# Fused attention and two feed-forward blocks: tiles that share slots with the first mixing blocks, mixing products behind the last y, x in six stores

## The chip, the cores and the metric

The kernel runs on one core of a Trainium2 chip. A core has engines with queues of their own that work in order: PE (TensorE, matrix products), DVE (VectorE), ACT (ScalarE), POOL (GpSimd) and SP (SyncE), which here only issues DMAs. DMAs issued by any of them run on 16 shared DMA engines. The metric is the time of one execution on the device, in microseconds (us).

## The reference, cut to what matters

```python
def _attn_ref(q, k, v, beta):                     # 4 x 8 x 768 x 48
    k_n = k / (np.linalg.norm(k, axis=-1, keepdims=True) + 1e-06)
    state = zeros((B, H, D, D))
    for t in range(S):
        y[:, :, t] = einsum('bhd,bhde->bhe', q[:, :, t], state)
        v_old = einsum('bhde,bhd->bhe', state, k_n[:, :, t])
        state = state + beta_t * einsum('bhd,bhe->bhde', k_n[:, :, t], v_t - v_old)
    return y
def _moe_ref(x, w_in, g_ln, w_sg, b_sg, w_out):   # x: 4 x 768 x 384
    h = gelu_tanh(x @ w_in)                       # 1024 columns
    u, v = h[..., :512], h[..., 512:]
    v_n = (v - mean(v)) / sqrt(var(v) + 1e-06) * g_ln
    v_s = einsum('ts,bsd->btd', w_sg, v_n) + b_sg[None, :, None]
    return x + (u * v_s) @ w_out
def _moe2_ref(x, mu_k, mu_r, w_k, w_v, w_r):
    xk = mu_k * x + (1 - mu_k) * x_prev; xr = mu_r * x + (1 - mu_r) * x_prev
    return sigmoid(xr @ w_r) * (relu(xk @ w_k) ** 2 @ w_v)
```

The result is the second block applied to the first block applied to the attention's output, with the heads side by side as 384 columns.

## The kernel before

Line numbers are those of the kernel before, as the profile gives them; those of the changed kernel are named as such. Every large product is made of three: each operand is split into a rounded high part and a low part (`split`, L106: ACT makes the high part at L111, DVE or POOL the low part at L114), and high x high, high x low and low x high are added in PSUM.

**Attention.** The sequence is cut into 12 chunks of 64 tokens, s = 0 to 11; two chunks are a group g (6 groups). The 32 pairs of batch and head are worked on in two halves, o = 0 and 1. Each (s, o) passes six stages: st_rq (the state's products rk and qk), st_d0, st_l, st_d1 (a triangular solve in blocks, with the inverse DT and the gram GL; u is copied out at L482, SQ at L500), st_s (the new state, L509, copied into SQ at L515) and st_y (y, L523, copied into yst at L528). The two halves run three stages apart. SQ is one tile for each of o, parity of s and half h. `run()` (L808) issues the pieces of two stages, then two ticks of a planner, then units of feed-forward work on PE. In a tick the planner issues a few DVE operations of the solver of the next group, of layer norm, or of weight conversion (raw weights come in by SP, pass ACT L155, DVE, POOL L168, ACT L111 and POOL and go out again as wk_dh, wk_dl and others). PE, DVE, ACT and POOL work in the order in which the program is written here; SP's order is made by a scheduler.

**From y to the first block.** At odd s the y of a group is stored into xT by eight DMAs (`store_x` L539: four at L543, four at L547), from SP; for group 5 half of them are issued by ACT. Some ticks later (LAGX = 6) the group's x is split (xh, xl) and its units run on PE: `v_units` (L595, evacuated by ACT at L604, normalised at L631, stored as vn_d at L636) and `u_units` (L647, ug at L651, stored as u_d).

**Mixing.** Behind the attention's loop (L823) new pools are opened. w_sg is loaded in 12 tiles wst (L844) and split into ws0 (columns of the first half, t = 0) and ws1; v_n comes back from memory as vst (L856) and is split into a ring of 9 pairs vh, vl. This list `ahead` is worked off one item per turn of a loop in which the last group's units run too. Then, for each batch b and half t, 4 x 6 blocks c of three mixing products each (`mix_mm` L931; 72 per half), a gate with u (loaded back by L923; DVE w at L944 and L946, split into gh and gl) and the projection (L142). `begin` (L966) issues products of c = 0 to 4 of all four d of (0,0) first. In this stage `side` puts the conversions of w_r and w_v between the gates. The scheduler orders all engines but PE here.

**Channel mix.** The last part (from 544.85 us) is the second block: 1440 products L142 in a row.

Of the kernel before, what the change touches and what calls it, by code (L numbers as in the profile page):

```python
# [20 lines left out]
P = 128  # L21
# [10 lines left out]
SV = 60  # L32
B0 = 1.4
# [3 lines left out]
RUN = (3, 1, 2)  # L37
# [11 lines left out]
LAGX = 6  # L49
LAGU = 2  # L50
SHARE = ((1, 4, 1), (1, 3, 1), (2, 5, 1))
NRAW = 3
NGL = 3
# [24 lines left out]
def fused_kernel(  # L78
# [139 lines left out]
    fp = fl.enter_context(fp)  # L218
    with ExitStack() as at:
# [14 lines left out]
        kTb = [ap1.tile([P, NPR, C], F32, name=f"kT{i}") for i in range(NKT)]  # L234
# [32 lines left out]
        Dm = ap1.tile([P, 32, 32], F32, name="Dm")  # L267
# [5 lines left out]
        SQ = [[[ap1.tile([P, 8, D + C], F32, name=f"SQ{o}{i}{h}") for h in range(2)]  # L273
# [14 lines left out]
        def gram(g, parts=((0, 64),)):  # L288

            GD = ap1.tile([P, 32, NU], F32, name="GD")  # L290
            GL = ap2.tile([P, NU, 32], F32, name="GL", bufs=NGL)
            GLs[g] = GL
# [28 lines left out]
        def product(a_off, a_dims, a_t, b_off, b_dims, b_t):  # L321

            sh = [d[1] for d in a_dims]
            tmp = ap1.tile([P, 1024], F32, name="tmp")
# [4 lines left out]
        def solver(g):  # L329

            NT = ap1.tile([P, 32, 32], F32, name="NT")
# [79 lines left out]
            DT = ap2.tile([P, NU, 32], F32, name="DT")  # L411
# [105 lines left out]
        def st_y(s, o):  # L517
            g, cur = s // 2, SQ[o][s % 2]
            yps = bank()
            for p in range(8):  # L520
                for h in range(2):
                    b0 = 64 * h
                    T.matmul(yps[b0:b0 + 64, p, :], lhsT=cur[h][:, p, 0:64],  # L523
                             rhs=cur[h][:, p, D:], start=True, stop=True)
# [14 lines left out]
        def store_x(g, o, yst):  # L539
            ts_ = slice(1 + P * g, 1 + P * g + P)  # L540
            for h in range(2):
                for i in range(2):
                    (nc.scalar if g == NG - 1 and i else nc.sync).dma_start(out=xT[D * h:D * h + D, 2 * o + i, :, ts_],  # L543
                                      in_=yst[64 * h:64 * h + D, 4 * i:4 * i + 3, :])
            for h, e, n, blk, row in ((0, 0, 32, 0, 96), (0, 32, 16, 1, 96),
                                      (1, 0, 16, 1, 112), (1, 16, 32, 2, 96)):
                (nc.scalar if g == NG - 1 and h else nc.sync).dma_start(  # L547
                                  out=xT[row:row + n, 2 * o:2 * o + 2, blk, ts_],
                                  in_=yst[64 * h + e:64 * h + e + n, 3:8:4, :])
# [60 lines left out]
        def ln_steps(g, b, v):  # L610
# [7 lines left out]
            if b % n == n - 1:  # L618
# [11 lines left out]
                def apply(i):  # L630
                    A.activation(vs[b0 + i], vs[b0 + i], AF.Identity, bias=nm[:, i:i + 1],  # L631
                                 scale=rs[:, i:i + 1])
                    if (b0 + i, g) == (0, NG - 1):
# [155 lines left out]
        def tick():  # L789
# [7 lines left out]
            late = point[0] >= LATE  # L797
            if jobs and len(running) < RUN[1 + late] and n % (2 if late else EVERY) == 0:
# [9 lines left out]
        def run(*bodies):  # L808
# [3 lines left out]
            for _ in range(2):  # L812
                tick()
            fill(UNITS)

        for s in range(12):
            for i in range(6):
# [299 lines left out]
```

## Time and profile before

| | |
|---|---|
| median of 3 runs | 798.91 us (798.80 to 802.15) |
| the profiled execution | 801.47 us, of which the span of its trace is 799.8 us |
| mean granted clock of PE | 0.974 of full speed |
| busy share | PE 90%, DVE 66%, ACT 45%, POOL 25% |
| chain that ended last | PE 58%, DVE 14%, DMA 8%, ACT 4%, issue 3%, POOL 3%, SP's queue 3% |

The stages in the profiled execution: the last group's solver ends and step 10 begins near 318 us, the last y starts at 358.81, the last units end at 384.2, mixing runs from 388.66, the first projection starts at 420.43, and the channel mix runs from 544.85 to the end. A busy share says how long an engine had an instruction in it. The chain follows back from the last instruction what released it. In a timeline a bracket at a row's end tells how long the engine was idle before the row, and which operation ended that; ACTq and SPq are the engines' issuing of DMAs.

### The profile page before, as it was taken

To read this page: it belongs to the slowest core of one execution; us is meant where nothing else is said; L and a number is where in the kernel's file an instruction comes from. 1 tells how busy PE (TensorE), PEld (TensorE's weight loads), DVE (VectorE), ACT (ScalarE), POOL (GpSimd) and SP (SyncE) were. 2 spreads that over 40 slices of the span, in tenths; PEclk is the share of its full clock that TensorE was granted. 3 is DMA by queue.
4 is the path that set the end of the run, shared out by engine and by line. 5 is a ranking of instruction groups with operands and counts; after the bars stand their busy time and mean duration, and the time that the engine had idled before them with its cause. 6 is when DMAs were issued, how large, how long until landed. Compare 5 with 4: busy or idle time off the path is not lost.

```text
span 799.8 us, 23669 instructions
## 1 busy us (share of the span) xinstructions
PE 719.3 (90%) x10126; PEld 652.8 (82%) x10126; DVE 524.5 (66%) x1087; ACT 360.6 (45%) x732; POOL 201.4 (25%) x246
## 2 busy tenths in 40 slices
PE   3478898998988989977789989999999999999998
PEld 3335677777877877766779978999999999999998
DVE  6989679698697797334367786458855555553442
ACT  3225455555645656654534232116644544542331
POOL 3254333344332434533406444101000000000000
PEclk9979999999999999997989999999999999999999
DMA  8313344364453455435994645138200000000000
GB/s 240 76 49 87 99 113 127 106 166 147 109 152 122 114 150 161 143 118 179 311 329 158 226 153 164 40 103 220 64 20 30 11 20 31 11 20 31 11 21 30
DMA packets 84713, 89.19 MB, mean 112 GB/s; under 512 B 25600, under 2 KB 68736, under 8 KB 84608
## 3 DMA queue, kind: packets, MB, share of 16 engines
q1 hardware_dynamic: 78976, 78.25, 32.7%
q0 software_dynamic: 4736, 9.04, 4.1%
q8 instruction: 79, 1.29, 0.7%
q10 hardware_dynamic: 896, 0.39, 0.2%
q14 instruction: 26, 0.21, 0.1%
HBM read 56.86 MB, written 26.08 MB: 104 GB/s over the span
## 4 chain that ended last, share of the span: by engine, by line
PE 58%; DVE 14%; DMA 8%; ACT 4%; issue 3%; POOL 3%; SPq 3%; ACTq 0%; DVEq 0%; POOLq 0%
PE ms L142 34%; PE ms L931 6%; PE ms L647 3%; PE ms L595 3%; DVE tmp L326 3%; PE rk L435 3%; PE ms L523 2%; DMA raw<-in_w_v_dram 2%; POOL na L168 1%; PE sps L509 1%; PE ms L686 1%; PE rk L489 1%; SPq L547 1%; DMA vst<-vn_d 1%; PE ms L303 1%
## 5 line engine op out<-in xcount | busy, mean ns | idle before, releaser
L142 PE MATMUL ms<-wvh,sh 128*128 128x384 f32 x192 | 64.9, 338 | 0.0
L142 PE MATMUL ms<-wvl,sh 128*128 128x384 f32 x192 | 64.9, 338 | 0.0
L142 PE MATMUL ms<-wvh,sl 128*128 128x384 f32 x192 | 64.8, 338 | 0.0
L142 PE MATMUL ms<-xm_lo,wkh 128*128 128x384 f32 x192 | 64.2, 334 | 0.0
L142 PE MATMUL ms<-xm_hi,wkh 128*128 128x384 f32 x192 | 64.2, 334 | 0.0
L142 PE MATMUL ms<-xm_hi,wkl 128*128 128x384 f32 x192 | 64.1, 334 | 0.0
L427 DVE TENSOR_TENSOR r<-vk,rk 128x384 f32<-128x384 f32 x40 | 22.0, 550 | 60.7 <-PE rk L489 21.4
L475 POOL TENSOR_SCALAR_AFFINE_SELECT SQ<-SQ 64x512 f32<-64x512 f32 x48 | 36.5, 760 | 93.9 <-ACT SQ L474 92.1
L168 POOL TENSOR_TENSOR na<-na,raw 128x256 int32<-128x256 int32 (+2 forms) x43 | 37.6, 876 | 80.2 <-DVE na L166 52.5
L114 DVE TENSOR_TENSOR sl<-r,sh 128x384 fp32r<-128x384 f32 x64 | 35.6, 556 | 30.2 <-ACT sh L111 30.2
L435 PEld LDWEIGHTS rk<-r,DT 32*32 32x32 f32 x1536 | 35.3, 105 | 20.6 <-DVE r L427 10.6
L435 PE MATMUL rk<-r,DT 32*32 32x48 f32 x1536 | 41.8, 203 | 10.7 <-DVE r L427 9.5
L111 ACT ACTIVATE sh<-r 128x384 fp32r<-128x384 f32 x64 | 33.5, 524 | 35.7 <-DVE r L1037 35.7
L305 PE MATMUL ms<-kT 64*32 64x64 f32 (+1 forms) x896 | 31.6, 229 | 12.1 <-issue 12.1
L1053 DVE TENSOR_TENSOR ob<-th,ms 128x384 f32<-128x384 f32 x24 | 13.2, 552 | 43.4 <-PE ms L142 43.4
L1037 DVE TENSOR_TENSOR r<-r 128x384 f32<-128x384 f32 x64 | 35.3, 551 | 9.7 <-ACT r L1036 9.7
L595 PE MATMUL ms<-wiv_hi,xh 128*128 128x512 f32 x72 | 30.2, 439 | 12.2 <-ACT GL L312 6.0
L303 PE MATMUL ms<-kT 64*32 64x64 f32 (+1 forms) x896 | 31.2, 229 | 11.1 <-DMA kT<-in_kt_d_dram 7.1
L1036 ACT ACTIVATE r<-ms 128x384 f32<-128x384 f32 x64 | 30.7, 480 | 20.7 <-PE ms L142 20.0
L500 ACT ACTIVATE SQ<-rk 64x384 f32<-64x384 f32 x48 | 23.3, 485 | 35.8 <-PE rk L435 33.3
L647 PE MATMUL ms<-xl,wiu_hi 128*128 128x256 f32 x144 | 39.3, 300 | 0.0
L111 ACT ACTIVATE gh<-w 128x384 fp32r<-128x384 f32 x32 | 16.6, 521 | 50.3 <-DVE w L946 50.3
(160 smaller groups left out, 2268.7 us busy)
## 6 DMA issues: line engine op xcount, KB each, us to landing
kT<-in_kt_d_dram SPq DMA_DIRECT2D x12, 512.0 KB, 4.3
u_d<-ug SPq DMA_DIRECT2D x24, 256.0 KB, 2.8
u<-u_d SPq DMA_DIRECT2D x16, 384.0 KB, 4.7
vn_d<-v SPq DMA_DIRECT2D x23, 256.0 KB, 3.2
vst<-vn_d SPq DMA_DIRECT2D x23, 256.0 KB, 3.5
SQ<-in_q_d_dram SPq DMA_DIRECT2D x48, 96.0 KB, 3.7
vk<-in_vk_dram SPq DMA_DIRECT2D x24, 192.0 KB, 3.5
vk<-in_vk_dram SPq DMA_DIRECT2D x12, 384.0 KB, 4.3
```

What stands on the lines that cost most here:

```text
L111: A.activation(hi, src, AF.Copy)
L114: eng_lo.tensor_tensor(lo, src, hi.bitcast(F32), op=ALU.subtract)
L142: T.matmul(pt, lhsT=a, rhs=b, start=(i == 0), stop=(i == n - 1))
L168: G.tensor_tensor(a.bitcast(I32), a.bitcast(I32), w_lo.bitcast(I32), op=ALU.add)
L303: T.matmul(gps[r:r + 32, p, c0:c1], lhsT=t[r:r + 64, u, 0:32], rhs=t[r:r + 64, u, c0:c1], start=True, stop=True)
L305: T.matmul(gps[r + 32:r + 64, p, c0:c1], lhsT=t[r:r + 64, u, 32:64], rhs=vw2(t, r, 64, u * C + 32, [(0, (c1 - c0) // 32), (1, 32)]), start ...
L435: T.matmul(RQs[o][b0:b0 + 32, p, 0:D], lhsT=DT[b0:b0 + 32, u0 + p, :], rhs=t[b0:b0 + 32, p, :], start=True, stop=True, skip_group_check=True)
L475: G.affine_select(out=pt, in_=pt, pattern=[[0, 8], [1, C]], compare_op=ALU.is_gt, fill=0.0, base=0, channel_multiplier=-1)
L595: T.matmul(vstat[g, b], lhsT=a[:, c], rhs=w[:, c], start=first, stop=last)
L647: T.matmul(vstat["u"][:, 2 * P * d:2 * P * d + 2 * P], lhsT=w[:, c, ds_], rhs=a[:, c].rearrange("p b t -> p (b t)"), start=first, stop=last)
L931: T.matmul(pt[:, :DM], lhsT=v[:, ds_], rhs=w[:, c], start=(c == 0 and i == 0), stop=(c == 5 and i == 2))
L1037: V.tensor_tensor(r, r, r, op=ALU.mult)
```

## The change

The changed kernel opens the pool `wq` of the mixing stage before the attention, with six slots w0h0 to w0l2 (12 KB a partition in all for the halves of ws0) and five ring slots g0 to g4. In the attention two of the four kT, tiles of GL and DT, the pair SQ of o = 0 and even s, and NT, GD, Dm and tmp of the solver lie in these slots. From the second stage of step 10 on, the slots are given to ws0 and the ring: `early_items`, one per tick, load four w_sg tiles and the four v_n tiles c = 0 to 3 of batch 0, and from step 11 the last two w_sg tiles of ws0; each item is a load into one of two rotating staging tiles (st0, st1) in one tick and its split in the next (EARLY = 1). v of group 4 is split directly into the ring from its v unit, as that of group 5 was. The first two loads were put by the scheduler at SP's rows 29 and 30, at the program's start.

`begin(0, 0, 5)` now stands directly behind the last y, ahead of the last group's splits and units. x is stored by six DMAs instead of eight (y's columns are laid in another order in PSUM for it), and ACT issues only three of them, those of (5,1), h = 1. A third weight conversion may run from tick 118 on (RUN, LASTP), the lag of the last group's splits is 4 and 1 ticks (LAGE). wk is loaded in six DMAs into the slots of ws0, and some tiles of the channel mix use the ring's slots.

The diff, cut to its core:

```diff
+EARLY = 1
-RUN = (3, 1, 2)
+RUN = (3, 1, 2, 3)
+LAGE = (4, 1)
+LASTP = 118
...
+    wq = ctx.enter_context(tc.tile_pool(name="wq", bufs=1, side="right", reuse_waits="tile"))
+    W0 = [f"w0{x}{i}" for i in range(3) for x in "hl"]
+    G0 = [f"g{i}" for i in range(5)]
+    def slot(tag, shape, dtype=F32):
+        return wq.tile(shape, dtype, name="s" + tag, tag=tag)
+    sts = [(stg, "st0"), (stg, "st1")]
+    def turn(tiles, shape, dtype=F32):
+        tiles.append(tiles.pop(0))
+        pool, tag = tiles[-1]
+        return pool.tile(shape, dtype, name=tag, tag=tag, bufs=1)
+    def staged(src, n):
+        x = turn(sts, [P, HF])[:, 0:n]
+        nc.sync.dma_start(out=x, in_=src)
+        return x
...
-        kTb = [ap1.tile([P, NPR, C], F32, name=f"kT{i}") for i in range(NKT)]
+        kTb = [slot(W0[i], [P, NPR, C]) if i < 2 else ap1.tile([P, NPR, C], F32, name=f"kT{i}")
+               for i in range(NKT)]
...
+        NT, GD, Dm = (slot(x, [P, 32, 32]) for x in G0[:3])
+        tmp = slot(G0[3], [P, 1024])
+        GLb = [slot(G0[4], [P, NU, 32]), slot(W0[2], [P, NU, 32]),
+               ap1.tile([P, NU, 32], F32, name="GL")]
+        DTb = [slot(W0[3], [P, NU, 32]), ap1.tile([P, NU, 32], F32, name="DT")]
...
-                after(LAGX, lambda: splits.append((g, o)))
+                after(LAGX if g < NG - 1 else LAGE[o], lambda: splits.append((g, o)))
...
+            queues = (nc.sync, nc.scalar if o + g == NG else nc.sync)
             for h in range(2):
-                for i in range(2):
-                    (nc.scalar if g == NG - 1 and i else nc.sync).dma_start(out=xT[D * h:D * h + D, 2 * o + i, :, ts_],
-                                      in_=yst[64 * h:64 * h + D, 4 * i:4 * i + 3, :])
+                queues[h].dma_start(
+                    out=vw2(xT, D * h, D, 2 * o * 3 * (S + 1) + 1 + P * g, [(S + 1, 6), (1, P)]),
+                    in_=yst[64 * h:64 * h + D, 0:6, :])
...
             for _ in range(2):
                 tick()
+                if early_items:
+                    early_items.pop(0)()
             fill(UNITS)
+        def to_ring(b, c, vst):
+            t = turn(rb, [P, 2 * HF], F32R)
+            vh, vl = ring[b, c] = (t[:, 0:HF], t[:, HF:2 * HF])
+            split(A, G if c % 3 else V, vst, vh, vl)
+        def into(hl, src):
+            x = staged(src, DM)
+            yield
+            split(A, V, x, *hl)
+        def ahead_of(*items):
+            gens = [x for x in items]
+            q = []
+            def step():
+                if gens:
+                    q.append(gens.pop(0)())
+                    next(q[-1])
+                if len(q) > EARLY or not gens and q:
+                    next(q.pop(0), None)
+            return [step] * (len(gens) + EARLY)
...
         for s in range(12):
             for i in range(6):
+                if (s, i) == (10, 1):
+                    open_ring()
+                    open_ws(0)
+                    open_ws(1)
+                    early_items += ahead_of(*[lambda c=c: ws_in(c) for c in range(4)],
+                                            *[lambda c=c: v_in(c) for c in range(4)])
+                if (s, i) == (11, 0):
+                    open_ws(2)
+                    early_items += ahead_of(*[lambda c=c: ws_in(c) for c in (4, 5)])
...
-        for i in range(3, 6):
-            run(stages[i](11, 1))
+        run(stages[3](11, 1))
+        for f in early_items:
+            f()
+        run(stages[5](11, 1))
...
+    begin(0, 0, CS[0])
     while later or splits or units or streams or opened[0]:
```

Three places in the order, the rows of the kernel before first and then those of the changed one. Names are the program's tiles with a number for each use.

ACT in step 10 (half 0): SQ is the state's tile, st0 and st1 are the staging tiles, sw0h1 is the high part of w_sg tiles 2 and 3, g0 the ring's pair for v tile 0, raw a weight under conversion. Before:

```order
L155 ACTIVATE raw_5495<-raw_5495 128x256
L111 ACTIVATE raw_5495<-na_5716 128x256 [waits Pool_49]
L500 ACTIVATE SQ000_111<-rk_5517 64x8x48 [waits PE_49]
L500 ACTIVATE SQ001_112<-rk_5517 64x8x48
L474 ACTIVATE SQ100_115<-qk_5750 64x8x64 [waits PE_49]
L474 ACTIVATE SQ101_116<-qk_5750 64x8x64
L515 ACTIVATE SQ010_113<-sps0_101 48x8x48 [waits PE_49]
L515 ACTIVATE SQ011_114<-sps0_101 48x8x48
L482 ACTIVATE u1_5837<-rk_5749 128x384 [waits DVE_49,PE_49]
L604 ACTIVATE v_5844<-ms_5795 128x512 [waits PE_49]
```

After:

```order
L113 ACTIVATE raw_5351<-na_5581 128x256 [waits Pool_49]
L113 ACTIVATE sw0h1_5456<-st0_5587 128x384 [waits DMAHW4_49]
L523 ACTIVATE sw0h2_122<-rk_5372 64x8x48 [waits PE_49]
L523 ACTIVATE sw0l2_123<-rk_5372 64x8x48
L497 ACTIVATE SQ100_126<-qk_5623 64x8x64 [waits PE_49]
L497 ACTIVATE SQ101_127<-qk_5623 64x8x64
L157 ACTIVATE raw_5430<-raw_5430 128x256
L113 ACTIVATE sw0h1_5456<-st1_5595 128x384 [waits DMAHW7_49]
L113 ACTIVATE raw_5430<-na_5667 128x256 [waits Pool_49]
L113 ACTIVATE g0_5683<-st0_5673 128x512 [waits DMAHW3_49]
L538 ACTIVATE SQ010_124<-sps0_104 48x8x48 [waits PE_49]
L538 ACTIVATE SQ011_125<-sps0_104 48x8x48
```

Three splits that wait for DMAs have come between the copies; the first stands ahead of the two copies SQ of L500 (L523 after). Behind these rows follow u (L505 after), the splits of g1 and g2, and only then v (L627 after).

SP at the same place: xT<-yst are the last x stores of (4,1), vk and vn_d a load and a store of the attention. Before:

```order
L547 DMA xT_63<-yst_5283 16x2x128 [waits DMAHW1_49]
L547 DMA xT_63<-yst_5283 32x2x128 [waits DMAHW2_49]
L246 DMA vk_5705<-in_vk_dram 64x768 [waits DMAHW3_49]
L247 DMA vk_5705<-in_vk_dram 128x768 [waits DMAHW4_49]
L636 DMA vn_d_67<-v_5447 128x512 [waits DMAHW5_49,Activation_49]
L195 DMA wk_dh_71<-raw_5430 128x256 [waits DMAHW6_49]
L195 DMA wk_dl_72<-na_5634 128x256 [waits DMAHW7_49,Pool_49]
L195 DMA wk_dh_71<-raw_5495 128x256 [waits DMAHW0_49,Activation_49]
L195 DMA wk_dl_72<-na_5716 128x256 [waits DMAHW1_49,Pool_49]
L151 DMA raw_5839<-in_w_k_dram 128x512 [waits DMAHW6_49,DMAHW2_49,DVE_49]
L151 DMA raw_6104<-in_w_k_dram 128x512 [waits DMAHW3_49,DMAHW0_49,DVE_49]
```

After:

```order
L571 DMA xT_63<-yst_5146 32x2x128 [waits DMAHW0_49]
L268 DMA vk_5570<-in_vk_dram 64x768 [waits DMAHW1_49]
L269 DMA vk_5570<-in_vk_dram 128x768 [waits DMAHW2_49]
L659 DMA vn_d_67<-v_5305 128x512 [waits DMAHW3_49,Activation_49]
L237 DMA st0_5587<-in_w_sg_dram 128x384 [waits DMAHW4_49,DVE_49]
L197 DMA wk_dh_71<-raw_5289 128x256 [waits DMAHW5_49]
L197 DMA wk_dl_72<-na_5495 128x256 [waits DMAHW6_49,Pool_49]
L237 DMA st1_5595<-in_w_sg_dram 128x384 [waits DMAHW7_49,DVE_49]
L197 DMA wk_dh_71<-raw_5351 128x256 [waits DMAHW0_49,Activation_49]
L197 DMA wk_dl_72<-na_5581 128x256 [waits DMAHW1_49,Pool_49]
L153 DMA raw_5664<-in_w_k_dram 128x512 [waits DMAHW5_49,DMAHW2_49]
L237 DMA st0_5673<-vn_d_67 128x512 [waits DMAHW4_49,DMAHW3_49,DVE_49]
```

The load of st0_5587, which ACT's split sw0h1 waits for, stands behind the x stores, vk and vn_d; the next load into the same tile, st0_5673, waits for DVE's part of that split.

PE behind the last y: xh and xl are the split x of a group, ms the product's bank, wiv and wiu the input weights, sw0h0 and sw0l0 the parts of w_sg tile 0, g0 the ring's pair. Before:

```order
L523 MATMUL ms_6363<-SQ110_117 64x64
L523 MATMUL ms_6363<-SQ111_118 64x64
L595 MATMUL ms_6431<-wiv_hi_90,xh_6393 128x512 [waits Activation_49]
L595 MATMUL ms_6431<-wiv_hi_90,xh_6393 128x512 x2
L595 MATMUL ms_6431<-wiv_lo_91,xh_6393 128x512 x3
L595 MATMUL ms_6431<-wiv_hi_90,xl_6394 128x512 [waits DVE_49]
L595 MATMUL ms_6431<-wiv_hi_90,xl_6394 128x512 x2
```

After:

```order
L546 MATMUL ms_6273<-SQ110_128 64x64
L546 MATMUL ms_6273<-SQ111_129 64x64
L670 MATMUL ms_6266<-xl_5802,wiu_hi_95 128x256 x3
L670 MATMUL ms_6266<-xh_5801,wiu_hi_95 128x256 x3
L670 MATMUL ms_6266<-xh_5801,wiu_lo_96 128x256 x3
L670 MATMUL ms_6266<-xl_5802,wiu_hi_95 128x256 x3
L937 MATMUL ms_6355<-sw0h0_5454,g0_5683 128x384
L937 MATMUL ms_6355<-sw0l0_5455,g0_5683 128x384
L937 MATMUL ms_6355<-sw0h0_5454,g0_5683 128x384
L937 MATMUL ms_6356<-sw0h0_5454,g0_5683 128x384
```

Before, the v units of group 5 follow the y and wait for its xh. After, 12 u products of group 4 and 60 mixing products, without a wait, stand between the y and these units.

## Rows read from the trace of the kernel before

**Rows 1.** The page: an engine's busy us, share and instructions.

```profile
PE 719.3 (90%) x10126; PEld 652.8 (82%) x10126; DVE 524.5 (66%) x1087; ACT 360.6 (45%) x732; POOL 201.4 (25%) x246
```

**Rows 2.** Stretches: length, busy PE, PEld, DVE, ACT, POOL, clock, DMA share, GB/s.

```profile
320.00:340.00 20.00, 18.70 (x405) 15.87 (x404) 6.51 (x16) 12.14 (x25) 10.76 (x15) 1.00 0.50 144
...
358.80:388.60 29.80, 20.63 (x140) 18.37 (x140) 12.24 (x28) 15.48 (x30) 12.73 (x21) 0.83 0.68 201
388.60:420.60 32.00, 29.10 (x128) 26.09 (x129) 19.40 (x35) 13.03 (x27) 5.14 (x5) 0.84 1.01 330
```

**Rows 3.** PE timeline, last y to first projection: start us, us, instructions, [idle before].

```profile
358.81 1.98 PE L523 MATMUL ms<-SQ 128*64 128x64 f32 x32 [3.38 <-ACT ug L651]
365.68 1.65 PE L595 MATMUL ms<-wiv_hi,xh 128*128 128x512 f32 x3 [4.90 <-ACT xh L111]
...
369.37 0.85 PE L595 MATMUL ms<-wiv_hi,xh 128*128 128x512 f32 x3
...
371.44 0.52 PE L647 MATMUL ms<-xh,wiu_hi 128*128 128x256 f32 x3
...
375.75 0.86 PE L595 MATMUL ms<-wiv_hi,xh 128*128 128x512 f32 x3
...
388.66 0.44 PE L931 MATMUL ms<-ws0h,vh 128*128 128x384 f32 x1 [4.33 <-ACT vh L111]
...
420.43 0.33 PE L142 MATMUL ms<-gh,wo_hi 128*128 128x384 f32 x1
```

**Rows 4.** Chain of waits in order of time: start us, us, what.

```profile
528.19 16.66 PE ms L931 x96
544.85 251.56 PE ms L142 x1440
```

**Rows 5.** SP timeline in step 10.

```profile
317.78 2.74 SPq L543 DMA_DIRECT2D xT<-yst  x4
320.57 2.54 SPq L547 DMA_DIRECT2D xT<-yst  x4
...
325.20 0.37 SPq L636 DMA_DIRECT2D vn_d<-v  x1
```

**Rows 6.** ACT timeline in step 10.

```profile
321.17 0.99 ACT L500 ACTIVATE SQ<-rk 64x384 f32<-64x384 f32 x2
...
324.17 0.47 ACT L482 ACTIVATE u<-rk 128x384 f32<-128x384 f32 x1
324.63 0.60 ACT L604 ACTIVATE v<-ms 128x512 f32<-128x512 f32 x1
326.65 0.60 ACT L528 ACTIVATE yst<-ms 128x512 f32<-128x512 f32 x1 [1.42 <-PE ms L523]
...
332.00 1.00 ACT L500 ACTIVATE SQ<-rk 64x384 f32<-64x384 f32 x2 [1.79 <-PE rk L435]
```

**Rows 7.** DMA issues: KB each, median us from issue to landing.

```profile
u<-u_d SPq DMA_DIRECT2D x16, 384.0 KB, 4.7
...
vst<-vn_d SPq DMA_DIRECT2D x23, 256.0 KB, 3.5
...
wst<-in_w_sg_dram SPq DMA_DIRECT2D x12, 192.0 KB, 4.4
raw<-in_w_out_dram SPq DMA_DIRECT2D x8, 192.0 KB, 2.9
```

**Rows 8.** Groups by line: busy us, mean ns of one, idle before.

```profile
L111 ACT ACTIVATE vh<-vst 128x512 fp32r<-128x512 f32 x23 | 13.9, 628 | 22.0 <-DMA vst<-vn_d 16.2 <-PE ms L931 5.7
L114 DVE TENSOR_TENSOR ws0l<-wst,ws0h 128x384 fp32r<-128x384 f32 x6 | 5.1, 853 | 10.3 <-ACT ws0h L111 10.3
```

**Rows 9.** ACT timeline in step 11: the x stores that ACT issues for (5,0).

```profile
349.80 1.57 ACTq L543 DMA_DIRECT2D xT<-yst  x2
351.41 1.38 ACTq L547 DMA_DIRECT2D xT<-yst  x2
```

**Rows 10.** PE timeline in a middle group: PE's wait for r.

```profile
180.34 0.87 PE L435 MATMUL rk<-r,DT 32*32 32x48 f32 x32 [2.30 <-DVE r L427]
```

More of the change, by code (lines that the diff above doesn't have):

```diff
@@ L272, in fused_kernel @@
                         base=0, channel_multiplier=1)
-        SQ = [[[ap1.tile([P, 8, D + C], F32, name=f"SQ{o}{i}{h}") for h in range(2)]
+        SQ = [[[ap1.tile([P, 8, D + C], F32, name=f"SQ{o}{i}{h}") if o or i else
+                vw(slot(W0[4 + h], [P, 1024]), 0, [(D + C, 8), (1, D + C)]) for h in range(2)]
                for i in range(2)] for o in range(2)]
@@ L861, in load_v, with mix_mm, begin @@
         to_ring(b, c, vsts.pop((b, c)))
-        if b == 0 and c < 2:
-            fetch_v(0, c + 3)
-    def to_ring(b, c, vst):
-        vh = vr.tile([P, HF], F32R, name="vh")
-        vl = vr.tile([P, HF], F32R, name="vl")
-        split(A, G if c % 3 else V, vst, vh, vl)
-        ring[b, c] = (vh, vl)
-    ahead = []
-    for i in range(5):
-        ahead += [lambda i=i: load_ws(0, i), lambda i=i: load_v(0, i)]
-    ahead.append(lambda: load_ws(0, 5))
-    for c in range(3):
-        fetch_ws(c)
-        fetch_v(0, c)
-    ahead += [lambda i=i: load_ws(1, i) for i in range(6)]
+    def mix_mm(pt, b, t, d, c):
+        ds_ = slice(d * P, d * P + P)
+        vh, vl = ring[b, c]
+        wh, wl = wsl[t][c]
+        for i, (v, w) in enumerate(((vh, wh), (vh, wl), (vl, wh))):
+            T.matmul(pt[:, :DM], lhsT=v[:, ds_], rhs=w, start=(c == 0 and i == 0),
+                     stop=(c == 5 and i == 2))
+    begun = {}
+    def begin(b, t, n):
+        for d in range(4):
+            begun[d] = (ps.tile([P, HF], F32, name="ms"), n)
+        for c in range(n):
+            for d in range(4):
+                mix_mm(begun[d][0], b, t, d, c)
     nc.sync.dma_start(out=b_sb, in_=b_sg.partition_broadcast(P))
+    ahead = ahead_of(*[lambda c=c: into(wsl[1][c], w_sg[c * P:(c + 1) * P, DM:2 * DM])
+                       for c in range(6)])
+    begin(0, 0, CS[0])
     while later or splits or units or streams or opened[0]:
@@ L924, in load_u @@
                               in_=u_d[b // 2, e, :, :, b % 2, t * DM:t * DM + DM])
-    def mix_mm(pt, b, t, d, c):
-        ds_ = slice(d * P, d * P + P)
-        vh, vl = ring[b, c]
-        wh, wl = ws[t]
-        for i, (v, w) in enumerate(((vh, wh), (vh, wl), (vl, wh))):
-            T.matmul(pt[:, :DM], lhsT=v[:, ds_], rhs=w[:, c], start=(c == 0 and i == 0),
-                     stop=(c == 5 and i == 2))
     def mix(b, t, d):
@@ L963, in fused_kernel @@
     load_u(0, 1)
-    begun = {}
-    def begin(b, t, n):
-        for d in range(4):
-            begun[d] = (ps.tile([P, HF], F32, name="ms"), n)
-        for c in range(n):
-            for d in range(4):
-                mix_mm(begun[d][0], b, t, d, c)
     for k, (b, t) in enumerate(halves):
```

102 lines of the change are left out of this document (55 added, 47 removed).

## The prediction

> **What bounds the kernel now.** I read the page's busy shares first: TensorE (PE) is busy nine tenths of the span [rows 1], so a gain has to come out of the tenth in which it is not, or out of a low clock. The chain of waits comes second. From 544.85 us it is one piece of 251.56 us of PE channel-mix products [rows 4]; nothing in the diff adds or removes a matmul there, so that third of the span stays. The table by stretches comes third and says where PE loses: between the start of the last y (358.8) and the start of the first projection (420.4) PE has two stretches with a granted clock of 0.83 and 0.84, is busy 20.63 of 29.80 us in the first, and in the second the DMA engines are full (share 1.01, 330 GB/s) [rows 2]. The PE timeline tells what it waits for there [rows 3]: 4.90 us for the split xh of the last group's x, then 4.33 us for the first split vh of the mixing stage, and short waits for weight splits after that. From 358.81 to 420.43 are 61.6 us.
>
> How much of it is work? Rates at full clock: nine v products from 369.37 to 371.44 are 0.23 us each, 36 u products from 371.44 to 375.75 are 0.12 us each [rows 3], 96 mixing products in 16.66 us are 0.1735 us each [rows 4]. Before, the place holds the y, 36 v, 72 u, 72 + 54 mixing products: 2 + 8.3 + 8.6 + 21.9 = 40.8 us of work in 61.6 us. So 20.8 us are waits and half clock, and that is what there is to win.
>
> **Part 1: 60 mixing products behind the last y.** In the order of the changed kernel the y is followed by 12 u products left over from group 4, then 60 mixing products of (0,0) whose operands were split during steps 10 and 11, so that they wait for nothing. Under them the last x lands, and the last group's units follow without the 4.90 us wait; the ring is full when they end, so the 4.33 us wait goes too. After the y starts: y 2.0 at the half clock of its row; 12 u products, between 1.4 (full clock) and 2.9 (half), I take 2.5, nearest to the y ahead of them, which ran slow; 60 x 0.1735 = 10.4; v 8.3; u 8.6; 12 mixing products of c = 5, 2.1; 54 of (0,1), 9.4. Sum 43.3 us. Next late is the first gating: the last u units end 31.8 us after the y starts, their stores and the reload of u stand behind them on SP's queue, a u load lands 4.7 us after its issue [rows 7], and four gatings follow on DVE and ScalarE (ACT). That comes about when the projection wants it; bounds 0 and 4 us, taken 1.5. So 44.8 instead of 61.6: **-16.8 us** (bounds -18.3 and -14).
>
> **Part 2: what steps 10 and 11 pay for it.** Ten loads into two staging buffers and eleven splits (six w_sg tiles, five v tiles, the fifth straight from its v unit) now stand in the queues of the last two steps. Two w_sg loads are issued at the program's start and cost only their split. The third is the expensive one. On ACT its split stands directly ahead of the copies SQ (L500 before), which the next state product waits for. ACT came to these at 321.17 [rows 6]. But its load stands on SP behind all x stores of (4,1), two vk loads and a vn_d store. SP issued eight x stores from 317.78 to 323.11, 0.66 us each, and the vn_d store at 325.20 with 0.37 us [rows 5]; two stores fewer bring its end to 325.57 - 1.32 = 324.25. Landing takes 2.9 us for a load of the same size from memory in the quiet attention stage, 4.4 us in the crowded mixing stage [rows 7]. At 320 to 340 us the DMA share is 0.50 [rows 2], so I take 2.9: 327.15, and ACT stands from about 321.2 to there, **6.0 us** (7.5 by the other row). Queued behind it are SQ and all of step 10's copies; PE, which works in a fixed order, waits for SQ.
>
> After that the pace is that of two buffers. A buffer's next load is issued only after both halves of its last split: for a v tile, landing 3.5 [rows 7], ACT 0.63 and DVE about 0.85 [rows 8], with issue some 5.3 us for a round. Followed by hand through ACT's queue: SQ at 327.7 and the affine copies to 329.9, second w_sg tile split by 330.8, the converted weight 332.4 (its wait on GpSimd kept), g0 by 333.2, u (L482) 334.5 instead of 324.17 or +10.3, g1 lands 335.3 and is split by 336, g2 lands 337.7 and is split by 338.4, then v (L604) at 338.4, where it was 324.63 [rows 6]: +13.8. Of that, five splits are 2.9 us, the rest waits. The state chain itself carries the +10.3 into the second half of step 10 and meets g3 there ahead of its SQ: about +11 to +12. Step 11 inserts three more splits, 1.7 us, and loses four x stores that ACT issued for (5,0), 1.57 + 1.38 = 2.95 us [rows 9], of which about half was ahead of a wait for PE anyway: together 0. The clock was full at 320 to 340 [rows 2]; after waits of this kind PE ran at the lower level in other places of the trace (the 0.83 above), so I add 1.5 us. **+13 us** on the start of the last y (bounds +7, rival one, and +20).
>
> The Trainium skill, "DMA: Bandwidth & Descriptors", section "Rules for kernel authors", says to issue a DMA early and wait for it late, since its fixed cost then overlaps with compute; one tick between load and split is against that rule, and the 2.9 us of the row speaks for the rule. Its section on the anatomy of one DMA fits 2.0 us plus the bytes at 436 GB/s, for GpSimd's path: that is an estimate of 2.45 us for a w_sg load and 2.6 us for a v tile, and by it the four landings in a row would be some 3 us shorter together, and the sum 792.6.
>
> **Part 3: the rest.** Six x stores for eight: in the middle groups PE's long wait once a group is for DVE's residual r, 2.30 us [rows 10], not for x, so 0 there; in steps 9 and 10 it is counted above. The shared slots (solver, gram, keys): they are taken over only after the last solver and gram have run, 0. In the mixing stage the conversion of w_r and w_v now starts later against PE, since PE arrives earlier by its own clock; it already made PE wait a few us there. I add 0.5 (bounds -1 and +4). The split of wk into six loads and the changed buffers of the channel mix: 0, for PE was without a gap there [rows 4].
>
> **Sum**: -16.8 + 13 + 0.5 = -3.3 us. The profiled execution took 801.47 us, 2.56 over the median of 798.91, and would become 798.2; against the median, the time to predict is 795.6. With the bounds of parts 1 and 3 it may be 2 us lower or 6 higher, with the landing times of part 2 some 5 lower or higher; its own range is 790 to 801.
>
> **Rivals.** *One: the waits fall into idle time.* ACT idled 1.42 us and 1.79 us between 324 and 332 waiting for PE [rows 6] and PE had slack in its units; if the rounds after the first stall hide there, only the 6.0 us and about 1 us of splits stay: +7 instead of +13, 789.6; and if the third load came in time too, -16.3 + 1, about 783. For it: neither PE nor ACT is full there. Against it: the copies stand in one queue, and the load's place behind the x stores is read from the order. *Two, slower: landings as in the crowded stage.* The change puts ten loads of 192 to 256 KB into steps in which x, vk, wk and u also move; if each of the four rounds in a row lands after 5.0 us rather than 2.9 or 3.5, the loss is 13 + 4 x 1.9 = 20.6 us, net +4.3, 803.2, and any PE time at the lower clock comes on top. It decides from landings of about 4.2 us (no gain left) and 5 us (slower by more than can be told from nothing). For it the 4.4 us row, against it the share of 0.50. *Three: the mixing products don't start behind the y*, because g4 or the third pair of w_sg tiles comes later than the y. Then PE waits in front of 60 products with the units queued behind them: some 5 us, 800.6. Against it: their splits stand on ACT well ahead of the last yst.
>
> **How the numbers follow.** The forecast 0.53, rival one 0.24, rival two 0.15, rival three 0.08. About 4 us (0.5%) is what a measurement of this kernel can tell from no change: faster means under 794.9, slower over 802.9. Forecast: 0.22 of its 0.53 lie under 794.9, 0.28 between, 0.03 above; rival one is faster but for 0.01; rival two slower in 0.12, rival three in 0.03. Faster 0.45, same 0.37, slower 0.18. The range that leaves out a tenth on either side: 784 to 804.
>
> **What would show it.** Right: an ACT wait of about 6 us for DMA in front of the third w_sg split at 321 us, and smaller ones before g1 and g2; the last y starting 10 to 16 us later, near 372; from there to the first projection about 45 us with mixing products at 0.17 us right behind the u products; equal length from the first projection on. Wrong: the last y starting under 365 (rival one), after 378 (rival two), a wait in front of the 60 products (three), or a long wait of PE for gl or wo in front of the first projection, which I priced at 1.5 us.

## The result, and the profile after

The changed kernel is slower: 810.46 us (median of 4 runs, 807.55 to 812.64) against 799.0 us, a ratio of 1.0132 with a 95% interval of 1.0089 to 1.0174. I had predicted 795.6, with 784 to 804 as the range. The profiled execution took 809.45 us, 8.0 more than the profiled one of before.

The trace gives three pieces. From the copy of y (9,1) to the copy of the last y, that is over steps 10 and 11: 318.84 to 380.83 us, 61.99, where before it was 316.21 to 360.82, 44.61: **+17.4**. From there to the channel mix: 171.85 instead of 184.03, **-12.2**. Before y (9,1): **+2.6**. Together 7.8, of the 7.9 between the spans of the two traces (807.7 and 799.8). The copies that bound the pieces, of the kernel before and then of the changed one (start us, us, instruction):

```profile
316.21 0.60 ACT L528 ACTIVATE yst<-ms 128x512 f32<-128x512 f32 x1 [0.48 <-PE ms L523]
...
360.82 0.60 ACT L528 ACTIVATE yst<-ms 128x512 f32<-128x512 f32 x1 [0.97 <-PE ms L523]
```

```profile
318.84 0.60 ACT L551 ACTIVATE yst<-ms 128x512 f32<-128x512 f32 x1
...
380.83 0.60 ACT L551 ACTIVATE yst<-ms 128x512 f32<-128x512 f32 x1 [1.62 <-PE ms L546]
```

The first piece, in ACT's timeline of step 10 (start us, us, instruction, idle time before it and what ended it), which answers [rows 6]:

```profile
323.70 0.42 ACT L113 ACTIVATE raw<-na 128x256 fp32r<-128x256 f32 x1 [2.09 <-POOL na L170]
331.65 0.52 ACT L113 ACTIVATE sw0h<-st 128x384 fp32r<-128x384 f32 x1 [7.53 <-DMA st<-in_w_sg_dram]
332.20 0.49 ACT L523 ACTIVATE sw0h<-rk 64x384 f32<-64x384 f32 x1
...
336.51 0.42 ACT L113 ACTIVATE raw<-na 128x256 fp32r<-128x256 f32 x1 [1.21 <-POOL na L170]
...
341.07 0.63 ACT L113 ACTIVATE g<-st 128x512 fp32r<-128x512 f32 x1 [1.59 <-DMA st<-vn_d]
341.60 0.58 ACT L627 ACTIVATE v<-ms 128x512 f32<-128x512 f32 x1
344.06 0.60 ACT L551 ACTIVATE yst<-ms 128x512 f32<-128x512 f32 x1 [1.88 <-PE ms L546]
...
351.81 0.99 ACT L523 ACTIVATE SQ<-rk 64x384 f32<-64x384 f32 x2 [2.06 <-PE rk L458]
```

ACT stands 7.53 us in front of the third w_sg split, and the two copies SQ (here named by the slots in which they lie, sw0h and sw0l) wait behind it. SP's timeline answers [rows 5]; the load that ACT waits for is its last row here and landed 3.86 us after its issue by the chain:

```profile
322.06 1.29 SPq L566 DMA_DIRECT2D xT<-yst  x2
323.40 2.53 SPq L571 DMA_DIRECT2D xT<-yst  x4
325.97 0.59 SPq L268 DMA_DIRECT2D vk<-in_vk_dram  x1
326.61 0.58 SPq L269 DMA_DIRECT2D vk<-in_vk_dram  x1
327.30 0.38 SPq L659 DMA_DIRECT2D vn_d<-v  x1
327.77 0.38 SPq L237 DMA_DIRECT2D st<-in_w_sg_dram  x1
```

ACT was ready at 324.12 (323.70 + 0.42). So 3.65 of its 7.53 us passed before SP had come through six x stores, two vk loads and a vn_d store to this load, and 3.88 until the load had landed.

PE in the same place (the state product and the y of (10,0), and behind them one of the v products), and then the stretches as in [rows 2]:

```profile
332.74 0.39 PE L532 MATMUL sps<-sw0h,vk 64*48 64x48 f32 x2 [8.59 <-ACT sw0h L523]
342.23 0.27 PE L546 MATMUL ms<-sw0h 128*64 128x64 f32 x1 [3.21 <-ACT v L627]
...
346.39 0.63 PE L618 MATMUL ms<-wiv_hi,xh 128*128 128x512 f32 x1
```

```profile
320.00:340.00 20.00, 10.32 (x175) 7.62 (x173) 6.15 (x12) 8.47 (x18) 8.88 (x9) 0.74 0.69 203
340.00:360.00 20.00, 16.12 (x316) 14.54 (x318) 8.14 (x16) 9.59 (x19) 8.65 (x12) 0.82 0.25 77
```

From 320 to 340 us PE is busy 10.32 us of 20 where it was 18.70, and the granted clock of the two stretches is 0.74 and 0.82 where it was 1.00 and 0.97.

The second piece. From the last y on, the chain of waits (start us, us, what) runs without a hole through the products that were moved there and half of the v units; behind these it goes, with shorter pieces between them, through three DMAs. The second fence shows PE's waits at the first projection, from the PE timeline, the third the chain's last row:

```profile
379.36 1.44 PE ms L546 x32
380.80 2.83 PE ms L670 x12
383.63 10.41 PE ms L937 x60
394.03 4.09 PE ms L618 x18
...
404.15 4.95 DMA st<-in_w_sg_dram
410.26 6.15 DMA st<-in_w_sg_dram
418.05 5.91 DMA u<-u_d
```

```profile
425.86 0.44 PE L144 MATMUL ms<-gh,wo_hi 128*128 128x384 f32 x1 [1.38 <-ACT gh L113]
...
429.00 0.69 PE L144 MATMUL ms<-gh,wo_hi 128*128 128x384 f32 x1 [1.40 <-ACT gh L113]
```

```profile
552.68 251.56 PE ms L144 x1440
```

Start of the last y on PE (379.36) to first projection (425.86): 46.5 us where [rows 3] have 61.6. The channel mix takes the same 251.56 us as [rows 4].

### The profile page after: what moved, and what is told of

The parts are those of the page before. It is cut to its first block, busy times and chain, and to the rows that moved or that the text cites. A ratio compares the mean times of both kernels' runs of the same rounds, so it can differ in the third digit from the quotient of the medians.

```text
span 807.7 us, 23622 instructions
## 1 busy us (share of the span) xinstructions
PE 726.1 (90%) x10126; PEld 661.5 (82%) x10126; DVE 525.0 (65%) x1087; ACT 360.8 (45%) x732; POOL 204.8 (25%) x250
## 4 chain that ended last, share of the span: by engine, by line
PE 64%; DVE 11%; DMA 7%; ACT 5%; POOL 3%; issue 2%; SPq 1%; DVEq 0%; POOLq 0%; ACTq 0%
PE ms L144 34%; PE ms L937 8%; PE ms L618 4%; PE ms L670 3%; PE rk L458 3%; PE ms L546 2%; DVE sg L350 2%; DMA st<-in_w_sg_dram 2%; PE sps L532 2%; PE rk L512 2%; PE ms L709 2%; POOL na L170 1%; DMA raw<-in_w_v_dram 1%; PE rk L482 1%; PE ms L328 1%
## 5 line engine op out<-in xcount | busy, mean ns | idle before, releaser
L144 PE MATMUL ms<-xm_hi,sw0h 128*128 128x384 f32 x192 | 64.1, 334 | 0.0
L144 PE MATMUL ms<-xm_lo,sw0h 128*128 128x384 f32 x192 | 64.1, 334 | 0.0
L144 PE MATMUL ms<-xm_hi,sw0l 128*128 128x384 f32 x192 | 64.1, 334 | 0.0
L116 DVE TENSOR_TENSOR sl<-sg,sh 128x384 fp32r<-128x384 f32 x64 | 35.7, 558 | 30.3 <-ACT sh L113 30.2
L937 PE MATMUL ms<-ws1h,g 128*128 128x384 f32 x192 | 50.2, 335 | 1.5 <-ACT ws1h L113 1.5
L937 PE MATMUL ms<-sw0h,g 128*128 128x384 f32 x192 | 50.1, 335 | 0.0
L350 DVE TENSOR_TENSOR sg<-sg,Yt 128x512 f32<-128x512 f32 (+10 forms) x78 | 44.1, 565 | 2.1
L1100 DVE TENSOR_TENSOR sg<-sg 128x384 f32<-128x384 f32 x64 | 35.4, 553 | 11.6 <-ACT sg L1099 11.5
L670 PE MATMUL ms<-xh,wiu_hi 128*128 128x256 f32 x144 | 40.1, 306 | 0.0
L670 PE MATMUL ms<-xh,wiu_lo 128*128 128x256 f32 x144 | 38.9, 298 | 0.0
```

Of the source, the lines that this page charges most:

```text
L116: eng_lo.tensor_tensor(lo, src, hi.bitcast(F32), op=ALU.subtract)
L144: T.matmul(pt, lhsT=a, rhs=b, start=(i == 0), stop=(i == n - 1))
L350: V.tensor_tensor(tv, vw(a_t, a_off, a_dims), vw(b_t, b_off, b_dims), op=ALU.mult)
L670: T.matmul(vstat["u"][:, 2 * P * d:2 * P * d + 2 * P], lhsT=w[:, c, ds_], rhs=a[:, c].rearrange("p b t -> p (b t)"), start=first, stop=last)
L937: T.matmul(pt[:, :DM], lhsT=v[:, ds_], rhs=w, start=(c == 0 and i == 0), stop=(c == 5 and i == 2))
L1100: V.tensor_tensor(r, r, r, op=ALU.mult)
```

## The experiments

In all of them two lengths are read from the one profile that each run has: **S**, from the copy of y (9,1) to the copy of the last y (44.61 us before, 61.99 in the changed kernel), and **M**, from there to the start of the channel mix (184.03 and 171.85). Ratios are to the kernel before, with 95% intervals. "W" is the theory that ACT's waits for the staged loads make the loss. In the expectations "theory E" says that the splits' own work makes it, and "theory S" that the shared slots or the new stores do; that letter has nothing to do with the length S.

**Splits without loads.**

```diff
+        if dry[0]:
+            dry[0] += 1
+            return dtile[dry[0] % 2][:, 0:n]
         x = turn(sts, [P, HF])[:, 0:n]
         nc.sync.dma_start(out=x, in_=src)
...
```

with `dry` set during steps 6 to 11 and `dtile` the two tiles filled in step 6.

> The changed kernel without the staged loads of steps 10 and 11 (ten, the two issued at the start among them): the eleven splits stay, and ten of them read a tile that was filled once in step 6, so part of the mixing operands is not the reference's. Theory W (ACT's waits for the staged loads make the loss): ACT's 7.5 us wait and those before the v tiles are gone, the last copy of y (380.8 in the changed kernel, 360.8 before) comes at 363 to 367, and the time is 793 +- 4. Theory E (the splits' own work on ACT, DVE and POOL in the queues makes it): the last copy of y still at 374 or later, time 803 or more.

Measured: 807.22 us, 1.0086 (1.0054 to 1.0118); S 61.10, M 172.36. My theory W fell here: all staged loads are gone and S is only 0.9 us shorter. The numbers are those of theory E, but the work of the splits did not make them. ACT's timeline shows a wait of nearly the same length a few rows further on: behind the two copies SQ that had waited before, in front of a converted weight, with the next copies SQ, u and v behind it:

```profile
331.68 0.42 ACT L113 ACTIVATE raw<-na 128x256 fp32r<-128x256 f32 x1 [6.80 <-POOL na L170]
```

S also hides something here. The copy of y (10,0) comes 21.51 us after that of y (9,1), 3.7 us earlier than in the changed kernel (25.22). Most of this is lost again in step 11, where PE ran at a granted clock of 0.50 from 355 to 363.

**One pair loaded ahead.** w_sg tiles 2 and 3 come into the idle slot g4.

```diff
+                if (s, i) == (9, 0):
+                    x = slot(G0[4], [P, 2, DM])
+                    for c in (2, 3):
+                        pre[c] = x[:, c - 2]
+                        nc.sync.dma_start(out=pre[c], in_=w_sg[c * P:(c + 1) * P, 0:DM])
...
```

> The changed kernel, but w_sg tiles 2 and 3 are loaded at the start of step 9 into the ring slot g4, which nobody uses then; all else stays. Theory W: the 7.5 us wait is gone, the v tiles are loaded a tick or two earlier in the two staging tiles, the last copy of y comes 8 to 11 us earlier (370 to 373), time 799 to 802. If the pace of two staging tiles sets the loss and not the one load behind the x stores, the waits move to g0 and g1 and no more than 4 us come back: 805 or more.

Measured: 806.76 us, 1.008 (1.0049 to 1.011); S 60.03, M 173.35. The time is that of the second reading, but for another reason: the long wait for the load is gone, and ACT waits 6.74 us for POOL's na instead, at the place of the run before.

**All early loads and splits back behind the last y.**

```diff
-                    early_items += ahead_of(*[lambda c=c: ws_in(c) for c in range(4)],
-                                            *[lambda c=c: v_in(c) for c in range(4)])
...
-                    early_items += ahead_of(*[lambda c=c: ws_in(c) for c in (4, 5)])
...
+    ahead = ahead_of(*[f for c in range(4) for f in (lambda c=c: ws_in(c), lambda c=c: v_in(c))],
+                     *[lambda c=c: ws_in(c) for c in (4, 5)],
...
-    begin(0, 0, CS[0])
...
     for f in ahead:
         f()
+    begin(0, 0, CS[0])
```

> The changed kernel with all early loads and splits moved back behind the last y and the 60 mixing products behind the last units, as before the change; shared slots, six stores, lags and the third conversion job stay. Theory W: the last copy of y at 359 to 364 (as before, 360.8, or the 1.5 us better that ACT's dropped issues give), time 797 to 803. Theory S (shared slots or the new stores cost in the attention, as the 2.9 us that the changed profile has by step 9 would say): the last copy of y at 364 or later, time 803 to 806.

Measured: 818.41 us, 1.0225 (1.019 to 1.0259); S 53.84, M 184.04. The time is beyond what either theory gave. S is 9.2 us too long with no early split in it at all, and ACT waits 7.39 us for POOL's na. What holds POOL is DVE, and what holds DVE is a store:

```profile
332.08 0.29 DVE L162 TENSOR_SCALAR na<-raw 128x256 uint32<-128x256 uint32 x1 [8.84 <-DMA wk_dl<-na]
```

That is a part of the change which I had passed over: with RUN's fourth entry a third weight conversion runs from tick 118. It needs a tile na, of which there are two, and both wait to be stored.

**Six stores alone**, on the kernel before.

```diff
...
-                for i in range(2):
-                    (nc.scalar if g == NG - 1 and i else nc.sync).dma_start(out=xT[D * h:D * h + D, 2 * o + i, :, ts_],
-                                      in_=yst[64 * h:64 * h + D, 4 * i:4 * i + 3, :])
+                queues[h].dma_start(
+                    out=vw2(xT, D * h, D, 2 * o * 3 * (S + 1) + 1 + P * g, [(S + 1, 6), (1, P)]),
+                    in_=yst[64 * h:64 * h + D, 0:6, :])
...
```

> The kernel before with the six x stores and the new column order of y alone. Theories W and E: 797 to 800, no difference but for what ACT no longer issues in step 11 (at most 1.5 us). Theory S: 802 or more.

Measured: 801.6 us, 1.0023 (0.9995 to 1.0052); S 42.73, M 182.46. The stores are not the loss. S is 1.9 us shorter, about what ACT no longer issues in step 11; the time shows none of it.

**A new theory, W2**: two waits stand side by side in step 10. ACT waits for a staged load, and DVE (then POOL, then ACT) for the store of a converted weight; both DMAs stand on SP behind the same x stores, so either wait alone costs most of what both cost. The next four runs take away one or both.

**Two conversions, staged loads kept.**

```diff
-LASTP = 118
+LASTP = 999
```

> The changed kernel with at most two weight conversions at a time (LASTP = 999), all else as changed. The runs so far show a second wait in step 10: the third conversion's first DVE operation waits for the store of an earlier wk_dl, which stands on SP behind the same x stores, and ACT then waits for POOL ahead of the copies SQ of L538. Theory W2 (two waits side by side, both ended by SP's queue): taking only this one leaves the 7.5 us wait for the staged load, the last copy of y comes 1 to 5 us earlier (376 to 380), time 804 to 809. If the third conversion alone made the loss: the last copy of y near 364, time 795 or less.

Measured: 812.01 us, 1.0138 (1.0086 to 1.019); S 62.76, M 177.11. Without the third conversion nothing is gained, as W2 says, for the wait for the load is there as ever:

```profile
327.78 0.52 ACT L113 ACTIVATE sw0h<-st 128x384 fp32r<-128x384 f32 x1 [6.84 <-DMA st<-in_w_sg_dram]
```

The last copy of y, at 378.43, is where W2 puts it; the time is 3 us above the 804 to 809 that I gave, because M is 5.3 us longer. Behind the last y four pieces of w_k are still loaded for conversion where the changed kernel has two. I take that to be the reason; no run tests it alone.

**Both waits away**: the first experiment with LASTP = 999.

> Both waits of step 10 taken away: no staged loads (ten of the eleven splits read a tile filled in step 6, so part of the mixing operands is not the reference's), and at most two conversions. Theory W2: nothing holds ACT in step 10 any more, the last copy of y comes at 363 to 367, time 790 to 797. Theory E (the work of the splits): last copy of y at 372 or later, time 801 or more.

Measured: 799.59 us, 0.9978 (0.9961 to 0.9996); S 48.78, M 176.35. S falls by 12.3 us against the run without loads and by 14.0 against the run with two conversions, though each of these alone had brought next to nothing. Up to the copy of y (10,0) alone, which no later stretch at half clock can blur, the times from y (9,1) are 25.22 us with both waits, 21.51 without the loads, 23.77 without the third conversion and 13.14 without both; before the change they were 10.44. The time is 2.6 us above the 790 to 797 that I gave, because M is again some 4 us longer than with a third conversion. S stays 4.2 us over that of the kernel before; I put this down to the work of eleven splits in these queues, which no run shows apart. In step 10 ACT runs from the third w_sg split to v without a gap:

```profile
320.39 0.51 ACT L113 ACTIVATE sw0h<-st 128x384 fp32r<-128x384 f32 x1
320.93 0.49 ACT L528 ACTIVATE sw0h<-rk 64x384 f32<-64x384 f32 x1
...
323.61 0.61 ACT L113 ACTIVATE g<-st 128x512 fp32r<-128x512 f32 x1
324.25 0.98 ACT L543 ACTIVATE SQ<-sps 48x384 f32<-48x384 f32 x2
```

**The pair ahead, two conversions**: the second experiment with LASTP = 999.

> w_sg tiles 2 and 3 loaded in step 9 into the slot g4, and at most two conversions; v tiles still loaded one tick ahead of their splits. Theory W2: the two long waits are gone, those for g0, g1 and g2 stay with 1 to 3 us each; last copy of y at 366 to 371, time 794 to 800. Theory E: 801 or more.

Measured: 808.94 us, 1.0109 (1.0082 to 1.0137); S 58.06, M 176.03. A miss: I had given the waits of the v tiles 1 to 3 us each. With the pair's wait gone, the load of g0, which stands on SP behind the same stores, makes the next one:

```profile
330.07 0.63 ACT L113 ACTIVATE g<-st 128x512 fp32r<-128x512 f32 x1 [5.48 <-DMA st<-vn_d]
...
334.90 0.63 ACT L113 ACTIVATE g<-st 128x512 fp32r<-128x512 f32 x1 [2.12 <-DMA st<-vn_d]
```

**All loads ahead, two conversions.** Here the v tiles are loaded ahead of the x stores too, three or four ticks before their splits.

```diff
+                    ws_get(0)
+                    ws_get(1)
+                    early_items += [lambda: (ws_put(0), get(0)), lambda: (ws_put(1), get(1)),
+                                    lambda: ws_put(2), lambda: ws_put(3),
+                                    lambda: (put(0), get(2)), lambda: (put(1), get(3)),
...
```

> As the run with the pair ahead and two conversions, and the v tiles' loads are issued three or four ticks ahead of their splits, the w_sg tiles 4 and 5 likewise: nothing of the change is left out. Theory W2: last copy of y at 362 to 367, from there to the first projection 44 to 47 us as in the changed kernel, time 788 to 795, faster than both. Theory E: 801 or more, like the runs without waits.

Measured: 800.01 us, 0.9983 (0.9962 to 1.0005); S 50.03, M 176.53. The last copy of y, at 366.64, is as W2 says, although one step of S, between the second and the third copy of y in it, takes 12.91 us at a granted clock of 0.66 where the next run takes 9.30 at 1.00. The time is a miss: it is that of the kernel before, because M is 4.7 us longer than in the changed kernel. From the last copy of y to the first projection it takes 49.9 us, not the 44 to 47 that I gave, with a wait of 3.29 us for a ws1 split.

**All loads ahead, the third conversion from tick 124** (the edit is against the run before).

```diff
-LASTP = 999
+LASTP = 124
```

> As the run with all loads ahead, but the third conversion is kept and may start from tick 124 instead of 118, so that its first DVE operation comes after the wk_dl store has landed. Theory W2: last copy of y at 365 to 368 as with two conversions, and the stretch from there to the channel mix is the 172 us of the runs with a third conversion (176 to 177 with two): channel mix from about 538, time 793 to 797, faster than both kernels. If the third conversion costs wherever it stands: last copy of y at 372 or later, time 800 or more.

Measured: 795.48 us, 0.9943 (0.9921 to 0.9966); S 47.69, M 172.67. This version computes everything and is faster than both kernels, by 0.6% and, by the two ratios, 1.9%; the time is as expected. The last copy of y, at 368.15, comes just after the 365 to 368 that I gave, since y (9,1) was 4.3 us later here than before. In its ACT timeline the splits of g0 and g1 stand between the copies without a wait:

```profile
326.17 0.49 ACT L523 ACTIVATE sw0h<-rk 64x384 f32<-64x384 f32 x1
...
328.42 1.15 ACT L113 ACTIVATE g<-st 128x512 fp32r<-128x512 f32 x2
329.60 0.99 ACT L538 ACTIVATE SQ<-sps 48x384 f32<-48x384 f32 x2
```

**The third conversion alone**, on the kernel before, from tick 118.

```diff
-RUN = (3, 1, 2)
+RUN = (3, 1, 2, 3)
+LASTP = 118
...
+            late += point[0] >= LASTP
```

> The kernel before with a third conversion from tick 118 alone. Theory W2: its wait for the wk_dl store behind the x stores (eight here) holds ACT and PE in step 10, the last copy of y is 8 to 10 us later (369 to 372), the stretch behind it some 0 to 5 us shorter, time 802 to 808. If the third conversion harms only together with the new slots or stores: 796 to 800.

Measured: 817.9 us, 1.0225 (1.0197 to 1.0254); S 58.12, M 185.21. One more entry in a planner's table, with the tick from which it counts, makes the kernel of before slower by more than the whole change does. Its rows name the chain on three engines: SP first, then the store that DVE waits for as the chain of waits has it (the first of the two wk_dl; it landed at 332.66), then DVE and ACT:

```profile
323.54 2.53 SPq L548 DMA_DIRECT2D xT<-yst  x4
...
328.70 0.45 SPq L196 DMA_DIRECT2D wk_dl<-na  x1
```

```profile
328.70 3.96 DMA wk_dl<-na
```

```profile
332.79 0.29 DVE L161 TENSOR_SCALAR na<-raw 128x256 uint32<-128x256 uint32 x1 [10.26 <-DMA wk_dl<-na]
```

```profile
335.20 0.42 ACT L112 ACTIVATE raw<-na 128x256 fp32r<-128x256 f32 x1 [8.82 <-POOL na L169]
335.64 0.98 ACT L516 ACTIVATE SQ<-sps 48x384 f32<-48x384 f32 x2
```

The wait and its place are W2's, the size is not: S is 13.5 us longer where I gave 8 to 10 for the last copy of y, with 10.4 of them up to the copy of y (10,0). The time lies 10 us above the 802 to 808 that I gave. I had also expected M to stay or to fall, and it rose by 1.2 us.

**The same from tick 124.**

> The kernel before with a third conversion from tick 124 alone. Theory W2: no wait, last copy of y at 360 to 363, time 795 to 801. If the third conversion costs wherever it stands, as in the run from tick 118: 802 or more.

Measured: 806.49 us, 1.0086 (1.0056 to 1.0117); S 46.94, M 186.85. Up to the copy of y (10,0) nothing is lost (10.44 us, as before), and the last copy of y, at 362.73, is where W2 puts it. The wait for the store is shorter and stands further on: DVE waits 4.38 us for a wk_dl behind that copy, then ACT 4.21 us for POOL, and S is 2.3 us longer. The time is a miss, in the range of the other theory: M is 2.8 us longer than before. PE waits 2.34 and 2.28 us for gh at the projection near 462 us, and its granted clock from 460 to 480 is 0.66 where it was 1.00. Why a conversion more in the attention costs the mixing stage of the kernel before, and helps that of the changed one, I did not find out.

**Mixing products back behind the units**, in the changed kernel.

```diff
-    begin(0, 0, CS[0])
     while later or splits or units or streams or opened[0]:
...
     for f in ahead:
         f()
+    begin(0, 0, CS[0])
```

> The changed kernel with the 60 mixing products put back behind the last group's units. All theories: the last copy of y at 378 to 383 as in the changed kernel. If the products behind the y give what the trace of the changed kernel shows (10.4 us of work in a stretch in which PE otherwise waits 4.9 us for xh and runs at half clock): 4 to 8 us slower than the changed kernel, 814 to 819; if the gain came from the early splits alone (full ring, no wait for vh): 810 or less.

Measured: 815.31 us, 1.018 (1.015 to 1.0209); S 61.24, M 176.34. The time is in the range that I gave for the first reading, but it is lost in another place. From the copy of the last y to the first projection this run takes 44.2 us, the changed kernel 45.0: with a full ring, PE waits 1.76 us for xh and nothing for the mixing products. The 4.5 us that M is longer are lost behind it, in waits for gh (3.23 and 1.10 us) and a granted clock of 0.74 between 420 and 440. So of the 12.2 us that M gained in the changed kernel, the splits ahead of time give some 7.7 (184.04 to 176.34, the third against the last experiment) and the new place of the products 4.5. These are differences of single profiles; M lies between 182.46 and 186.85 in the five versions without early splits.

## Why the prediction was wrong, point by point

**Part 1, the mixing products behind the last y: right, somewhat too large.** Predicted 44.8 us from the last y to the first projection, measured 46.5: -15.1 instead of -16.8. The 60 products took 10.41 us, as worked out from the rate of [rows 4], and neither xh nor vh was waited for. Rival three, in which they would have started late, did not come. What the sum lacked is PE's wait of 1.47 us for a ws1 split, which stood in no term. The reload of u, priced at 1.5 us, holds PE for 1.38 us ahead of the first projection, in front of gh; 1.40 us more for gh come behind it, and the products then run at half clock until 434 us.

**Part 2, steps 10 and 11: the step that failed.** Predicted +13, measured +17.4. The first wait was sized from the right rows, but its load was issued 3.65 us after ACT was ready (3.05 by the sum) and landed after 3.86 us (2.9 taken, 4.4 was the other row), and it came to 7.53 instead of 6.0. The estimate from the Trainium skill, "DMA: Bandwidth & Descriptors", anatomy section, 2.45 us for this load, was farther off. The Trainium skill's rule on the same page, section "Rules for kernel authors", to issue a DMA early and wait for it late, is borne out: with two conversions S is 62.76 us with one tick between load and split and 50.03 with all loads ahead. ACT's queue was followed well: against y (9,1), v came 14.3 us late, where 13.8 stood. The error came after that. "The state chain itself carries the +10.3" was wrong: PE takes its instructions in a fixed order, and the y of (10,0) needs the bank that ACT's copy v frees, [3.21 <-ACT v L627] above. So everything behind it on PE was late by what v was late by, not by what u was: yst of (10,0) 14.8 and SQ of (10,1) 17.2 where I had written 11 to 12. Of the 2.4 us between these two much is clock: v products took 0.43 us each (346.39 to 346.81 and on) where [rows 3] have 0.23. From SQ of (10,1) to the end of step 11 nothing was lost, as predicted.

**The wait that I did not see.** The third conversion has no term in the prediction. The rows for raw_5430 stand in my own excerpt of the order, between the copies of step 10, and I kept "its wait on GpSimd" at what it was elsewhere. In the order of DVE that conversion writes a tile that an earlier store must have left. In the changed kernel this wait hides under the other one (ACT's 1.21 us for POOL are what is seen), so it added little to the sum. But it decides on the second form of rival one, in which the third load comes in time: with the first wait gone, the second holds the copies that follow (SQ from sps, u and v), and S stays at 60 to 61 us, as the first two runs show. The first form, in which only the 6.0 us stay and the later rounds hide, is refuted by the changed kernel itself: v came 14.3 us late.

**Part 3: too low.** From the first projection to the channel mix the changed kernel took 126.8 us, before 124.4: +2.4 for the 0.5 that I gave. And y (9,1) was 2.6 us late already. I don't count that to the change: over the twelve experiments y (9,1) came between 1.3 us earlier and 4.3 us later than before, and in the profile of the changed kernel this delay arose at 288 us, where PE ran at the lower clock after a wait that both kernels have (2.44 us for r; the rows stand in the last section).

Together: 4.4 in part 2, 1.7 in part 1, 1.9 in part 3 and 2.6 ahead of it all are 10.6 of the 11.3 us between the forecast of -3.3 and the measured +8.0; the rest is rounding and where the last y is read. So part 2 is the largest error, but it alone would not have taken the time out of the range: with 17.4 in place of 13 the sum would have been +1.1 us, about 800. **Rival two** had the right sign and a wrong place: the landing times (3.8 us in the median for both kinds of staged load) were below the 4.2 from which I said it decides. Its sum has a slip: from 2.9 or 3.5 to 5.0 us are 2.1 or 1.5, so the four rounds make about 7 us and not 4 x 1.9 = 7.6; nothing hangs on it.

## What to carry to other kernels

When a load is put one tick ahead of its use, count what its queue has to issue first: of a wait of 7.5 us here, half was the queue's other DMAs and half the landing. When a wait is taken away, look at which other wait on the same queue ends at the same time: two that stand side by side showed 1 us of S or none when one was removed, and 12 to 14 us more when the other went too. And a number in a planner's table that lets one more job run is an edit like any other: follow its first instruction to the buffer it writes, and to the store that must free it.

## What the runs showed of the hardware that was not expected

PE's clock fell for longer than the wait that came before it. Behind the 8.59 us wait in step 10 the v products start 0.43 us apart at 337 us and still at 346.39, and the u products are 0.12 us apart again only from 349.36; one more wait, of 3.21 us, lies between. Over the 40 us from 320 the granted clock was 0.74 and 0.82.

The same wait need not have the same effect. All fourteen profiles, of these kernels and experiments, have PE's wait for r near 288 us, 2.43 or 2.44 us long. Behind it the 32 products rk took 0.87 us in twelve of them, the kernel before among them, and 1.49 us in two, the changed kernel and the run with all splits late. Before and after:

```profile
288.23 0.87 PE L435 MATMUL rk<-r,DT 32*32 32x48 f32 x32 [2.44 <-DVE r L427]
```

```profile
288.40 1.49 PE L458 MATMUL rk<-r,sw0l 32*32 32x48 f32 x32 [2.44 <-DVE r L450]
```

From this row to the copy of y (9,1) it took 27.98 to 29.22 us in the twelve and 30.44 and 30.76 us in the two. What decides between the two cases the traces do not show. So a difference of one to three microseconds between two of these profiles can lie in the clock, and is no sign of the edit.
